# An induced-attention and ELU feed-forward kernel: one unsplit pair of a block becomes a split one on GpSimd, and the other's subtraction moves to ScalarE

## The chip, the cores and the metric

The kernel runs as one program on one core of a Trainium2 chip. The metric is the time of one execution on the device, in microseconds (us); lower is better. A core has TensorE (PE in the profile, with its weight loads as PEld), VectorE (DVE), ScalarE (ACT), GpSimd (POOL) and SyncE (SP, which issues the transfers here). Each engine works through its own list of instructions in order, and waits on semaphores for the others.

## The reference

Two parts follow each other. The first attends from 32 inducing points to all 12480 tokens of a batch, and then from the tokens back to the 32 results. The second is a feed-forward layer with ELU on all 4 x 12480 tokens.

```python
# attention: B, N, m, C = 4, 12480, 32, 128
h = mab(I, x)          # softmax(scale * I @ x^T) @ x, per batch
x = mab(x, h)          # softmax(scale * x @ h^T) @ h
# feed-forward: d_model 128, d_ff 2048 (weights are float64 inputs)
h = x @ w_in
g = np.where(h > 0.0, h, np.exp(np.minimum(h, 0.0)) - 1.0)
return (g @ w_out).astype(np.float32)
```

## The kernel before, in words

**Blocks, pairs and units.** The tokens of a batch are cut into 25 blocks: 15 of 512 tokens and 10 of 480 (`GROUPING`), 100 blocks in all. d_ff is 16 chunks of 128; two chunks are a pair, so a block has 8 pairs. One pair of one block is a unit, numbered n = 0 to 799; n modulo 8 is its place in the block.

**One unit.** `ffn_in` (L560, L568): two matmuls fill a tile `ph` of [128, 2, T] in PSUM with h + 1, and ScalarE writes e = exp(ph - 1) to SBUF. `ffn_mid` (L574): VectorE forms min(max(ph, 1), e), which is ELU + 1. `ffn_split` (L583 to L597) subtracts the 1 and, for most pairs, cuts the value into a rounded upper part `gh` and a lower part `gl`, each of which one fast matmul can carry. `ffn_out` (L618) adds the products with w_out into the block's `po` in PSUM. After the eighth pair VectorE transposes `po` (L625), and SP stores it.

**Three kinds of pair.** `PLAN` gives a letter to each of the 8 pairs; `PLAN_CALM` replaces it for the last 17 blocks of the last batch (block 8 on), where no next batch is being prepared. The kinds differ in who makes what:

- D: ELU + 1 stays in `ph`; ScalarE writes `gh` (L583), VectorE writes `gl` (L586) and only then is `ph` free. Six matmuls for the output.
- P: ELU + 1 goes to `e`, so `ph` is free after L574; ScalarE writes `gh`, then GpSimd subtracts 1 in place (L591) and writes `gl` (L596). Six matmuls.
- N: ELU + 1 goes to `e`; GpSimd subtracts 1 in place (L591). There is no split: two matmuls in full float32 with `wo_n`, each of which the profile records twice.

**Buffers.** The pools rotate: 3 tiles of `ph` (PSUM), 5 of `e` (`EB`), 4 of `gh` (`GHB`), 3 of `gl` (`GLB`). A split pair's `gl` takes the buffer of the third split pair before it, and so waits for that pair's output matmuls. Which `ph` tile a unit takes is settled when the program is built.

**What sets the order.** TensorE's order is written out by hand (`manual_schedule`): input matmuls of unit n, then output matmuls of unit n - 5 (`LAG`), then n + 1 and n - 4. Attention steps of this batch and of the next (`attend`, `first_half`) are put between units at written-out times. The order on VectorE, ScalarE and GpSimd is chosen when the program is built, by a scheduler with a timeline of its own; it decides, for example, whether a D pair's L586 stands ahead of a later unit's L574.

## Time and profile before

| what | value |
|---|---|
| median of 3 runs (lowest to highest) | 1762.04 us (1761.57 to 1762.32) |
| profiled execution, its span | 1761.6 us, 1759.5 us |
| granted TensorE clock, mean | 0.987 |
| PE busy / PEld busy | 1659.5 us (94%) / 1177.4 us (67%) |
| DVE busy | 1551.8 us (88%) |
| ACT busy | 1425.0 us (81%) |
| POOL busy | 1331.7 us (76%) |

Busy means that an instruction was recorded as running. A matmul's record is longer than the time until the next one can start, since they are pipelined, so the distance between starts tells more than a matmul's length. The chain of waits is the work followed back from the last instruction: at each step to what released it. "Idle before <- X" names the instruction whose end let the waiting one start.

### The profile page before, as it was taken

Reading aid. Unit: us, or ns where it says so; the run is one execution under the profiler, and the core shown is the slowest. Engines: PE = TensorE matmul, PEld = TensorE weight load, DVE = VectorE, ACT = ScalarE, POOL = GpSimd, SP = SyncE. Lnnn points to the kernel's source line nnn. Section 1 sums busy time; section 2 is a strip of 40 time slices with the busy share of each in tenths; the row PEclk is TensorE's granted clock in tenths of the full one; section 3 lists DMA queues with packets and bytes.
Section 4 is the critical chain, followed back from the end, with each engine's and each line's share of the span. In section 5 each row is a group of like instructions: output and inputs, shape, how many; then the busy total and the mean of one; then the engine's idle time right before and its main releaser. Section 6 shows DMA issues by size and latency. Waiting matters only on the chain.

```text
span 1759.5 us, 22797 instructions
## 1 busy us (share of the span) xinstructions
PE 1659.5 (94%) x7480; PEld 1177.4 (67%) x7480; DVE 1551.8 (88%) x1635; ACT 1425.0 (81%) x1662; POOL 1331.7 (76%) x955
## 2 busy tenths in 40 slices
PE   6699999999999999999999999999999999989897
PEld 4356666677766766767676666667777776667676
DVE  6899989888999898889899998988899988888886
ACT  6778888788887887878787888878888888888786
POOL 3978877777787777777787787777778887766665
PEclk9599999999999999999999999999999999999999
DMA  7362323323234224232225232321221211111111
GB/s 248 65 98 48 66 56 51 73 44 78 53 54 72 60 49 77 41 53 71 66 42 88 44 65 60 52 49 41 58 53 18 45 22 32 25 23 34 21 17 17
DMA packets 384757, 98.12 MB, mean 56 GB/s; under 512 B 364864, under 2 KB 370784, under 8 KB 384384
## 3 DMA queue, kind: packets, MB, share of 16 engines
q1 hardware_dynamic: 384640, 96.68, 28.4%
q8 instruction: 59, 0.97, 0.2%
q14 instruction: 58, 0.48, 0.1%
HBM read 48.94 MB, written 25.56 MB: 42 GB/s over the span
## 4 chain that ended last, share of the span: by engine, by line
PE 73%; DVE 12%; ACT 5%; issue 3%; POOL 3%; DMA 3%; SPq 0%; DVEq 0%; ACTq 0%; POOLq 0%
PE po L618 51%; PE ph L560 18%; DVE gl L586 4%; ACT e L568 3%; DVE ph L574 2%; DVE e L574 2%; DVE xT L241 2%; ACT gh L583 1%; PE ps_hh L369 1%; PE ps_t L485 1%; PE ps_s L293 1%; POOL gl L596 1%; DMA w_raw<-in_moe_w_in_dram 1%; DMA xq<-in_x_dram 1%; DMA xm<-in_x_dram 1%
## 5 line engine op out<-in xcount | busy, mean ns | idle before, releaser
L568 ACT ACTIVATE e<-ph 128x1024 f32<-128x1024 f32 (+1 forms) x800 | 803.5, 1005 | 241.3 <-PE ph L560 237.9
L591 POOL TENSOR_SCALAR e<-e 128x1024 f32<-128x1024 f32 (+1 forms) x483 | 495.4, 1031 | 354.2 <-ACT gh L583 309.0
L596 POOL TENSOR_TENSOR gl<-e,gh 128x1024 fp32r<-128x1024 f32 (+1 forms) x300 | 704.4, 2348 | 19.8 <-PE po L618 0.9
L574 DVE SCALAR_TENSOR_TENSOR e<-ph,e 128x1024 f32<-128x1024 f32 (+1 forms) x483 | 571.5, 1187 | 75.1 <-ACT e L568 73.1
L560 PE MATMUL ph<-stk,hw 128*128 128x512 f32 (+1 forms) x1600 | 563.0, 433 | 60.7 <-DVE gl L586 43.7
L618 PE MATMUL po<-gh,wo_h 128*128 128x512 f32 (+1 forms) x1234 | 481.7, 390 | 10.5 <-ACT e L568 6.5
L618 PE MATMUL po<-gh,wo_l 128*128 128x512 f32 (+1 forms) x1234 | 478.9, 388 | 0.0
L560 PEld LDWEIGHTS ph<-stk,hw 128*128 128x128 f32 x1600 | 289.9, 189 | 247.1 <-issue 92.8
L574 DVE SCALAR_TENSOR_TENSOR ph<-ph,e 128x1024 f32<-128x1024 f32 (+1 forms) x317 | 378.3, 1196 | 47.7 <-ACT e L568 46.4
L586 DVE SCALAR_TENSOR_TENSOR gl<-ph,gh 128x1024 fp32r<-128x1024 f32 (+1 forms) x317 | 375.8, 1185 | 40.4 <-PE po L618 25.9
L618 PE MATMUL po<-gl,wo_h 128*128 128x512 f32 (+1 forms) x1234 | 379.1, 388 | 2.8 <-POOL gl L596 2.8
L618 PE MATMUL po<-e,wo_n 128*128 128x512 f32 (+1 forms) x732 | 336.3, 582 | 0.0
L583 ACT ACTIVATE gh<-e 128x1024 fp32r<-128x1024 f32 (+1 forms) x300 | 311.1, 1037 | 26.6 <-DVE e L574 21.9
L583 ACT ACTIVATE gh<-ph 128x1024 fp32r<-128x1024 f32 (+1 forms) x317 | 318.0, 1003 | 11.5 <-DVE ph L574 9.7
L618 PEld LDWEIGHTS po<-gh,wo_h 128*128 128x128 f32 x1234 | 232.4, 188 | 64.5 <-ACT s L302 5.6
L618 PEld LDWEIGHTS po<-gl,wo_h 128*128 128x128 f32 x1234 | 232.4, 189 | 49.1 <-POOL gl L596 3.9
L618 PEld LDWEIGHTS po<-gh,wo_l 128*128 128x128 f32 x1234 | 232.7, 189 | 46.3 <-issue 0.2
L618 PEld LDWEIGHTS po<-e,wo_n 128*128 128x128 f32 x732 | 138.1, 189 | 97.3 <-issue 84.0
L625 DVE STREAM_TRANSPOSE o<-po 128x512 f32<-128x512 f32 (+1 forms) x100 | 69.3, 693 | 11.8 <-PE po L618 11.8
L241 DVE STREAM_TRANSPOSE xT<-xq 128x1024 f32<-128x1024 f32 (+2 forms) x39 | 45.2, 1160 | 0.0
L369 PE MATMUL ps_hh<-xm,e 128*32 128x128 f32 (+2 forms) x872 | 33.3, 296 | 8.4 <-DVE bias L326 2.3
L369 PEld LDWEIGHTS ps_hh<-xm,e 128*32 128x32 f32 (+2 forms) x872 | 25.4, 117 | 20.1 <-issue 12.4
(94 smaller groups left out, 582.3 us busy)
## 6 DMA issues: line engine op xcount, KB each, us to landing
xm<-in_x_dram SPq DMA_DIRECT2D x32, 512.0 KB, 4.4
out_dram<-o SPq DMA_DIRECT2D x240, 64.0 KB, 2.0
xq<-in_x_dram SPq DMA_DIRECT2D x84, 128.0 KB, 3.6
out_dram<-o SPq DMA_DIRECT2D x160, 60.0 KB, 2.0
stk<-ahi SPq DMA_DIRECT2D x118, 64.0 KB, 2.0
xq<-in_x_dram SPq DMA_DIRECT2D x60, 120.0 KB, 3.4
stk<-ahi SPq DMA_DIRECT2D x80, 60.0 KB, 2.0
stk<-alo SPq DMA_DIRECT2D x59, 64.0 KB, 2.0
```

Source lines behind the costliest of these rows:

```text
L241: tc.keep_in_program_order(nc.vector.transpose(t, xq.rearrange("p u d -> p (u d)")))
L293: nc.tensor.matmul(ps[j * Q : (j + 1) * Q, :T], indT, block_xT(b, g0 + j), start=True, stop=True,)
L369: nc.tensor.matmul(ps[c * Q : (c + 1) * Q, :C], st["e", g][:np_, u * Q : (u + 1) * Q], st["xm", g, u - u % UP][:np_, u % UP, :], start=(u ...
L560: nc.tensor.matmul(ph[:, i], state[b]["hw"][:, f * P : (f + 1) * P], stacks[b, k], start=True, stop=True,)
L568: nc.scalar.activation(e, ph, AF.Exp, bias=-1.0)
L574: nc.vector.scalar_tensor_tensor(out=v["g"], in0=v["ph"], scalar=1.0, in1=v["e"], op0=ALU.max, op1=ALU.min)
L583: nc.scalar.activation(v["gh"], v["g"], AF.Copy, bias=-1.0)
L586: nc.vector.scalar_tensor_tensor(out=v["gl"], in0=v["g"], scalar=-1.0, in1=v["gh"].bitcast(F32), op0=ALU.add, op1=ALU.subtract,)
L591: nc.gpsimd.tensor_scalar(out=v["e"], in0=v["e"], scalar1=-1.0, scalar2=1.0, op0=ALU.add, op1=ALU.mult)
L596: nc.gpsimd.tensor_sub(v["gl"], v["e"], v["gh"].bitcast(F32))
L618: nc.tensor.matmul(po[:, :T], w, g, start=(cp == 0 and i == 0), stop=(cp == NCP - 1 and i == len(parts) - 1),)
L625: nc.vector.transpose(o.rearrange("p u d -> p (u d)"), po[:, :T])
```

## The change

`PLAN` goes from PDNPDPND to PDPDPNPD: three P, three D and two N become four P, three D and one N, in another order. `PLAN_CALM` goes from PDNPDPDD to PDPDDNPD: three P, four D and one N as before, in another order. The N pair's subtraction of 1 goes from GpSimd to ScalarE (a Copy with bias -1, in place on `e`); the P pair's instructions are the same. The tables `CHUNKS_N` and `CHUNKS_S` follow the plans: `wo_n` now holds two chunks and not four.

```diff
-PLAN = "PDNPDPND"
-PLAN_CALM = "PDNPDPDD"
+PLAN = "PDPDPNPD"
+PLAN_CALM = "PDPDDNPD"
...
                 out=v["gl"], in0=v["g"], scalar=-1.0, in1=v["gh"].bitcast(F32),
                 op0=ALU.add, op1=ALU.subtract,
             )
-        else:
+        if how == "N":
+            nc.scalar.activation(v["e"], v["e"], AF.Copy, bias=-1.0)
+        if how == "P":
             nc.gpsimd.tensor_scalar(
                 out=v["e"], in0=v["e"], scalar1=-1.0, scalar2=1.0, op0=ALU.add, op1=ALU.mult
             )
-        if how == "P":
             v["gl"] = glp.tile(shape, F32R, tag="gl", name=f"gl_{n}")
             nc.gpsimd.tensor_sub(v["gl"], v["e"], v["gh"].bitcast(F32))
```

The lines behind the edit move by one: L591 is now the ScalarE Copy, L593 and L597 are GpSimd's two steps, L619 the output matmuls and L626 the transpose of `po`.

The order on VectorE is shown for block 37, units 296 to 303, a block of 512 tokens in the second batch (a name such as `ph_297_6324` is the tile `ph` of unit 297). L574 writing `e` is a P or N pair, L574 writing `ph` a D pair, L586 a D pair's lower part. Before:

```order
L574 SCALAR_TENSOR_TENSOR e_296_6309<-ph_296_6306,e_296_6309 128x1024
L586 SCALAR_TENSOR_TENSOR gl_295_6320<-ph_295_6295,gh_295_6318 128x1024
L574 SCALAR_TENSOR_TENSOR ph_297_6324<-ph_297_6324,e_297_6327 128x1024
L574 SCALAR_TENSOR_TENSOR e_298_6344<-ph_298_6341,e_298_6344 128x1024
L586 SCALAR_TENSOR_TENSOR gl_297_6355<-ph_297_6324,gh_297_6353 128x1024
L574 SCALAR_TENSOR_TENSOR e_299_6365<-ph_299_6362,e_299_6365 128x1024
L574 SCALAR_TENSOR_TENSOR ph_300_6371<-ph_300_6371,e_300_6374 128x1024
```

And now, from the same unit on (L626 is the transpose of the block before):

```order
L574 SCALAR_TENSOR_TENSOR e_296_6603<-ph_296_6600,e_296_6603 128x1024
L586 SCALAR_TENSOR_TENSOR gl_295_6614<-ph_295_6581,gh_295_6612 128x1024
L574 SCALAR_TENSOR_TENSOR ph_297_6618<-ph_297_6618,e_297_6621 128x1024
L574 SCALAR_TENSOR_TENSOR e_298_6638<-ph_298_6635,e_298_6638 128x1024
L586 SCALAR_TENSOR_TENSOR gl_297_6645<-ph_297_6618,gh_297_6643 128x1024
L574 SCALAR_TENSOR_TENSOR ph_299_6652<-ph_299_6652,e_299_6655 128x1024
L626 STREAM_TRANSPOSE o_1_11_6680<-po_1_11_6555 128x512
L574 SCALAR_TENSOR_TENSOR e_300_6672<-ph_300_6669,e_300_6672 128x1024
```

The lower part of unit 297 (place 1) stands at the same place. Counting split pairs back from it, its buffer was unit 293's before (296, 295, 293; 294 was an N) and is unit 294's now (296, 295, 294). Behind it now stand the D pair of unit 299 and the transpose, and then unit 300, whose `ph` tile unit 302 takes.

The order on ScalarE in the same block, from the middle to the end; L568 is the exponential, L583 an upper part. Before:

```order
L568 ACTIVATE e_300_6374<-ph_300_6371 128x1024
L583 ACTIVATE gh_299_6389<-e_299_6365 128x1024
...
L568 ACTIVATE e_301_6400<-ph_301_6397 128x1024
L583 ACTIVATE gh_300_6410<-ph_300_6371 128x1024
L568 ACTIVATE e_302_6417<-ph_302_6414 128x1024
L583 ACTIVATE gh_301_6426<-e_301_6400 128x1024
L568 ACTIVATE e_303_6434<-ph_303_6431 128x1024
L568 ACTIVATE e_304_6443<-ph_304_6440 128x1024
```

And now:

```order
L568 ACTIVATE e_301_6697<-ph_301_6694 128x1024
L583 ACTIVATE gh_299_6687<-ph_299_6652 128x1024
...
L583 ACTIVATE gh_300_6707<-e_300_6672 128x1024
L568 ACTIVATE e_302_6715<-ph_302_6712 128x1024
L591 ACTIVATE e_301_6697<-e_301_6697 128x1024
L568 ACTIVATE e_303_6728<-ph_303_6725 128x1024
L583 ACTIVATE gh_302_6737<-e_302_6715 128x1024
L568 ACTIVATE e_304_6745<-ph_304_6742 128x1024
```

Before, two exponentials followed each other where a pair was an N; now each exponential has a second ScalarE step in its block, an upper part or the Copy. On GpSimd the order before was two steps for each P and one for each N; now it is two steps for each of the four P pairs, evenly in every second unit.

## The prediction, on record before the result was known

> **What bounds the kernel now.** I read the cores first, then the chain of waits, then the busy time by stage.

> ```profile
> core 0: 1759.5 us, clock 0.987
> ...
> PE 73%; DVE 12%; ACT 5%; issue 3%; POOL 3%; DMA 3%; SPq 0%; DVEq 0%; ACTq 0%; POOLq 0%
> ...
> 200.00:1300.00 1100.00, 1072.98 (x4863) 755.47 (x4862) 989.52 (x1023) 899.34 (x1020) 854.40 (x584) 1.00 0.31 58
> 1300.00:1455.00 155.00, 155.00 (x622) 112.98 (x621) 141.44 (x140) 133.55 (x147) 130.85 (x89) 1.00 0.19 33
> 1460.00:1740.00 280.00, 251.28 (x1027) 187.32 (x1026) 238.32 (x230) 229.13 (x251) 190.85 (x125) 0.99 0.14 24
> ...
> ACT e L568 <- PE ph L560: 237.9, 281, 2.3
> ```

> The windows' columns are PE, PEld, DVE, ACT, POOL, granted clock, DMA share and GB/s. PE is busy 97.5% of the long middle (1072.98 of 1100) and all of 1300 to 1455; DVE 90 to 91%, ACT 82 to 86%, POOL 78 to 84%. The chain is PE for 73%, and ScalarE's main wait is for PE. So PE bounds the blocks up to 1455 us; the calm blocks behind have PE at 90% (251.28 of 280) and another bound, below.

> **What the change takes from PE.** The chain shows units back to back, a split pair's output as x6 and an N pair's as x4 (records), with the input matmuls between:

> ```profile
> 702.04 1.38 PE po L618 x6
> 703.89 1.40 PE po L618 x6
> 705.74 1.72 PE po L618 x4
> 707.46 0.47 PE ph L560 x2
> 707.92 1.38 PE po L618 x6
> ...
> 787.81 1.30 PE po L618 x6
> 789.54 1.61 PE po L618 x4
> 791.59 1.31 PE po L618 x6
> ```

> At 512 tokens a split unit takes 1.85 us from start to start (702.04 to 703.89) and an N unit 2.18 (705.74 to 707.92): the swap saves 0.33. At 480 it saves 2.05 - 1.73 = 0.32. The plan is used in 83 blocks (three batches and 8 blocks): 53 of 512, 30 of 480. 53 x 0.33 + 30 x 0.32 = **27 us less on PE**. The calm plan keeps one N and saves nothing. [...]

> **What it adds to ScalarE.** Per plan block one upper part and one Copy, both reading SBUF like `gh<-e`:

> ```profile
> 700.29 1.03 ACT L568 ACTIVATE e<-ph 128x1024 f32<-128x1024 f32 x1 [0.21 <-PE ph L560]
> 701.22 1.02 ACT L583 ACTIVATE gh<-ph 128x1024 fp32r<-128x1024 f32 x1
> 702.12 1.03 ACT L568 ACTIVATE e<-ph 128x1024 f32<-128x1024 f32 x1
> 703.03 1.07 ACT L583 ACTIVATE gh<-e 128x1024 fp32r<-128x1024 f32 x1
> 703.99 1.03 ACT L568 ACTIVATE e<-ph 128x1024 f32<-128x1024 f32 x1
> ...
> 708.02 1.03 ACT L568 ACTIVATE e<-ph 128x1024 f32<-128x1024 f32 x1 [1.16 <-PE ph L560]
> ```

> Back to back an exponential takes 0.92, `gh<-ph` 0.90, `gh<-e` 0.96. A D and a P unit together need 3.70 (700.29 to 703.99), what PE takes for two split units (2 x 1.85). Today ScalarE recovers at each N: 1.16 idle at 708.02. The new N unit has a second step too, so what is left in a block is about 2.18 - 1.88 = 0.3. Per block ScalarE gets 1.9 more, 83 x 1.9 = 158, and 17 x 0.93 = 16 in the calm blocks: busy 1425 to 1599. The cover is the 237.9 us that it waits for PE. **Bounds:** nothing, if that cover holds in place; at most what the rival below gives. Queued behind ScalarE are the exponentials that release `ph`; there is not much room, so I take a third of the upper bound of 53 (worked out with that rival): **+18 us**.

> **What it adds to GpSimd.** One P more, two N steps fewer:

> ```profile
> 704.19 1.05 POOL L591 TENSOR_SCALAR e<-e 128x1024 f32<-128x1024 f32 x1 [0.16 <-ACT gh L583]
> 705.32 2.38 POOL L596 TENSOR_TENSOR gl<-e,gh 128x1024 fp32r<-128x1024 f32 x1
> 707.65 1.07 POOL L591 TENSOR_SCALAR e<-e 128x1024 f32<-128x1024 f32 x1
> ```

> A P costs 3.46 (704.19 to 707.65), an N 1.05: +1.36 a block, busy 1332 to about 1427. Four P need 13.8 of the some 15.1 us that a block's PE work lasts, one in every second unit (3.46 of 3.70). It fits: zero, unless attention steps pile up on it.

> **The buffers of the lower parts: the added wait.** Before, every D of the plan had an N among the three units ahead, so its `gl` buffer came from the unit four back, whose output was long done. Now places 1, 2, 3 and 4 take the buffer of the unit three back. For P pairs and place 3 that is no later than their own work. For place 1 it is. Unit 297 is a D at place 1:

> ```profile
> 701.41 0.63 PE L560 MATMUL ph<-stk,hw 128*128 128x512 f32 x2
> ...
> 706.19 1.21 DVE L586 SCALAR_TENSOR_TENSOR gl<-ph,gh 128x1024 fp32r<-128x1024 f32 x1
> 707.32 1.21 DVE L574 SCALAR_TENSOR_TENSOR e<-ph,e 128x1024 f32<-128x1024 f32 x1
> 709.08 1.23 DVE L574 SCALAR_TENSOR_TENSOR ph<-ph,e 128x1024 f32<-128x1024 f32 x1 [0.55 <-ACT e L568]
> 710.22 0.71 DVE L625 STREAM_TRANSPOSE o<-po 128x512 f32<-128x512 f32 x1
> 710.85 0.67 DVE L360 STREAM_TRANSPOSE e<-s 128x512 f32<-128x512 f32 x1
> ```

> Its L586 ran at 706.19; the output of unit 294 ended at 707.46 (the chain's row above). Waiting for it, L586 starts 1.3 later, and VectorE, in order, stands. Lay it out from unit 297's input at 701.58 in the chain's timing as 0: output of 294 ends 5.88; L586 to 7.06 (1.13 to the next start); unit 299's L574 to 8.20; the transpose to 8.83 (0.63); unit 300's L574 ends 10.05 (1.22). Unit 302 takes that `ph` tile and is due at 4 x 1.85 + 2.18 = 9.58. PE stands **0.5 us**. That order (L586, place 3, transpose, place 4) is in 27 of the 83 blocks. In 14, place 3 comes ahead of L586, and the same sum gives 0.26. In the others nothing: without the transpose it ends at 9.42. 27 x 0.5 + 14 x 0.26 = **+17 us**. Bounds: 0, where attention matmuls stand between; 42, if all 83 lose 0.5.

> **The calm blocks.** They show today what such a buffer does:

> ```profile
> DVE gl L586 <- PE po L618: 15.2, 13, 1.3
> PE ph L560 <- DVE gl L586: 28.7, 31, 3.1
> ...
> 1581.91 0.70 PE L560 MATMUL ph<-stk,hw 128*128 128x480 f32 x2 [1.41 <-DVE gl L586]
> 1586.06 0.70 PE L560 MATMUL ph<-stk,hw 128*128 128x480 f32 x2 [0.24 <-DVE gl L586]
> ...
> 1582.71 0.97 ACT L568 ACTIVATE e<-ph 128x960 f32<-128x960 f32 x1 [0.80 <-PE ph L560]
> 1583.71 1.17 DVE L574 SCALAR_TENSOR_TENSOR ph<-ph,e 128x960 f32<-128x960 f32 x1 [0.21 <-ACT e L568]
> ```

> (The first two rows are waits in 1460 to 1740.) A block loses 1.41 + 0.24. In the changed program place 6 takes, in 15 of 17 blocks, the `ph` tile of place 5 just ahead of it: input to the end of L574 is 1584.88 - 1581.91 = 2.97, against a unit of 1.73, so PE would stand 1.3. Per block 0.35 less, 5 us; two D in a row may cost some back (bounds -5 to +10). I take **-3 us**.

> **Sum**, against the profiled execution's 1761.6 (median 1762.0, so no correction): 1761.6 - 27 + 18 + 17 - 3 = **1767 us**.

> **Rivals.**

> *The relief stays, the waits are absorbed.* Attention matmuls stand between units in most blocks and hide 0.5, and ScalarE's idle time covers its two steps. For it: PE is the bound and ScalarE waits for it, 237.9 us. Against it: DVE stays at 90% of a shorter block. 1761.6 - 27 - 3 with half of the 17: **1740 us**.

> *ScalarE becomes the bound.* Windowed rows give its load:

> ```profile
> L568 ACT ACTIVATE e<-ph 128x1024 f32<-128x1024 f32 x301 | 309.0, 1027 | 93.0 <-PE ph L560 92.7
> L568 ACT ACTIVATE e<-ph 128x960 f32<-128x960 f32 x224 | 217.7, 972 | 69.0 <-PE ph L560 67.7 <-issue 0.2
> ```

> 525 exponentials in 200 to 1300 are 65.6 blocks, 16.76 us each, 13.7 of it ScalarE's; with 1.87 more, 15.57. The highest share that any of the three elementwise engines keeps over a stretch is DVE's 141.44 of 155, 91.2%. Were that the most for ScalarE too, a block takes 17.07, 0.31 more, 83 x 0.31 = 26: **1788 us**, which is 53 above 1735, the time without any stall. It decides as soon as ScalarE cannot go above 93% (15.57 of 16.76). For GpSimd the same reckoning, (13.02 + 1.36) / 0.912 = 15.8, is under 16.76: no bound.

> *The bubble is in every block.* The lower part's wait costs 0.5 in all 83, 42 in place of 17: **1791 us**. Speaking for it: the calm rows repeat theirs in block after block. [...] Against it: only 27 blocks have the bad order.

> **How the numbers follow.** The forecast of a small loss has 0.46 (its own range 1759 to 1782), the absorbed case 0.34, ScalarE as bound 0.10, the bubble everywhere 0.10. 0.2%, 3.5 us, is about what a measurement of this kernel tells from no change. Faster: 0.31 of the absorbed case and 0.03 of the forecast, 0.34. Same: 0.03 and 0.10, 0.13. Slower: 0.33 + 0.20, 0.53. The range reaches from 1737, where nearly all stalls are absorbed, to 1800, just above the two dear cases.

> **What would show it.** N records of L619 in the plan halve; ScalarE's busy time near 1599 and GpSimd's near 1427. The wait of VectorE's lower part for PE's output, now 15.2 in the calm stretch, appears in the plan blocks, some 40 to 80 times of about 1 us. PE's waits at the input matmuls name VectorE's L574. If ScalarE bounds, its wait for PE falls to a few tens of us and PE waits on exponentials. The prediction is wrong if PE keeps 97.5% in the middle with fewer N (absorbed), or if GpSimd's `gl` appears among PE's waits.

## The result, and the profile after

| | before | after |
|---|---|---|
| median (lowest to highest) of 4 runs | 1762.03 us (1761.57 to 1762.32) | 1785.77 us (1784.76 to 1786.33) |
| ratio, with its 95% interval | | 1.0136 (1.0121 to 1.0151) |
| span of the profiled execution, granted clock | 1759.5 us, 0.987 | 1783.8 us, 0.988 |

The changed kernel is 23.7 us slower. The forecast was 1767, slower by 5; the time lies inside the range of 1737 to 1800, 19 us above the forecast and close to the two dear rivals (1788 and 1791).

The page of the changed kernel, busy time of each engine, and the shares of the chain of waits:

```profile
span 1783.8 us, 23710 instructions
...
PE 1653.0 (93%) x7646; PEld 1200.5 (67%) x7646; DVE 1548.6 (87%) x1635; ACT 1586.2 (89%) x1843; POOL 1428.9 (80%) x938
...
PE 58%; DVE 18%; ACT 10%; issue 8%; POOL 4%; DMA 1%; DVEq 0%; SPq 0%; ACTq 0%; POOLq 0%
```

PE's share of the chain fell from 73% to 58%, and VectorE's and ScalarE's rose from 12 and 5 to 18 and 10. PE has a little less to do than before (1653.0 against 1659.5 busy), and the chain hangs on it less.

The groups of the page that belong to the swap (busy time, mean ns of one, idle time ahead):

```profile
L619 PE MATMUL po<-gl,wo_h 128*128 128x512 f32 (+1 forms) x1400 | 430.0, 388 | 4.7 <-POOL gl L597 4.6
...
L619 PE MATMUL po<-e,wo_n 128*128 128x512 f32 (+1 forms) x400 | 183.6, 581 | 0.0
L591 ACT ACTIVATE e<-e 128x1024 f32<-128x1024 f32 (+1 forms) x100 | 103.1, 1031 | 13.6 <-DVE e L574 13.5
```

Before, the first two rows had x1234 and x732. So the change does what it says: 83 units more are split, each with two such records, 83 fewer are full float32, and 100 Copies have come to ScalarE.

Where the 24 us came from is read by stage. I call the time from the first input matmul of unit 0 to that of unit 664 the **plan stage** (the 83 blocks that use `PLAN`), and what is behind it the **rest**. The starts of those two units, before and then after:

```profile
68.54 1.22 PE L560 MATMUL ph<-stk,hw 128*128 128x512 f32 x2 [9.35 <-DVE stk L528]
...
1455.57 1.03 PE L560 MATMUL ph<-stk,hw 128*128 128x512 f32 x2
```

```profile
68.52 1.22 PE L560 MATMUL ph<-stk,hw 128*128 128x512 f32 x2 [9.01 <-DMA hw<-hw_l]
...
1482.76 0.63 PE L560 MATMUL ph<-stk,hw 128*128 128x512 f32 x2
```

The plan stage went from 1387.0 to 1414.2 us (+27.2), the rest from 303.9 to 301.0 (-2.9). Two windows over just the two plan stages (columns as in the prediction), before and after:

```profile
68.52:1455.52 1387.00, 1351.06 (x5981) 950.48 (x5982) 1249.93 (x1282) 1139.58 (x1288) 1089.17 (x751) 1.00 0.30 56
```

```profile
68.52:1482.72 1414.20, 1343.79 (x6148) 973.82 (x6149) 1247.23 (x1282) 1286.62 (x1455) 1204.33 (x752) 1.00 0.30 55
```

PE's busy time there fell by 7.3, and the time in which it stood rose from 35.9 to 70.4. What it waited for shows in the waits of the changed kernel (engine, tile and line waited for; us in total, times, longest):

```profile
ACT e L568 <- PE ph L560: 92.7, 156, 2.5
...
PE ph L560 <- DVE e L574: 61.3, 85, 1.7
...
DVE gl L586 <- PE po L619: 58.7, 60, 1.3
...
POOL gl L597 <- PE po L619: 29.9, 45, 1.4
```

VectorE's lower part now waits for PE's output 60 times, 58.7 us (before 26 times, 25.9 us, half of them in the calm blocks), and PE waits at its input matmuls for VectorE's L574, 61.3 us (before 6.1). Counted off in the order of the records, 39 of VectorE's 44 waits in the plan stage are at place 1; 26 of GpSimd's 40 there, 26.4 us, are at place 2. ScalarE's wait for PE fell from 237.9 to 92.7, but was not used up. Block 37, the one that the prediction laid out, shows the two waits together. Its VectorE rows, from the L574 of unit 298 to those of units 300 and 301 (one row, x2):

```profile
715.15 1.23 DVE L574 SCALAR_TENSOR_TENSOR e<-ph,e 128x1024 f32<-128x1024 f32 x1 [0.18 <-ACT e L568]
717.66 1.23 DVE L586 SCALAR_TENSOR_TENSOR gl<-ph,gh 128x1024 fp32r<-128x1024 f32 x1 [1.28 <-PE po L619]
718.80 1.22 DVE L574 SCALAR_TENSOR_TENSOR ph<-ph,e 128x1024 f32<-128x1024 f32 x1
719.93 0.71 DVE L626 STREAM_TRANSPOSE o<-po 128x512 f32<-128x512 f32 x1
720.56 2.32 DVE L574 SCALAR_TENSOR_TENSOR e<-ph,e 128x1024 f32<-128x1024 f32 x2
```

and PE's row for the input of unit 302:

```profile
721.89 0.70 PE L560 MATMUL ph<-stk,hw 128*128 128x512 f32 x2 [0.67 <-DVE e L574]
```

L586 waits 1.28 for the output of the unit three back, the three instructions queued behind it (unit 299's L574, the transpose, unit 300's L574) run late without a gap, and PE stands 0.67 until the last of them has freed `ph`. Predicted were 1.3 and 0.5.

### The profile page after: what moved, and what is told of

Its sections match the earlier page's. It is cut to its first block, busy times and chain, and to the rows that moved or that the text cites. A ratio compares the mean times of both kernels' runs of the same rounds, so it can differ in the third digit from the quotient of the medians.

```text
span 1783.8 us, 23710 instructions
## 1 busy us (share of the span) xinstructions
PE 1653.0 (93%) x7646; PEld 1200.5 (67%) x7646; DVE 1548.6 (87%) x1635; ACT 1586.2 (89%) x1843; POOL 1428.9 (80%) x938
## 4 chain that ended last, share of the span: by engine, by line
PE 58%; DVE 18%; ACT 10%; issue 8%; POOL 4%; DMA 1%; DVEq 0%; SPq 0%; ACTq 0%; POOLq 0%
PE po L619 38%; PE ph L560 15%; DVE e L574 6%; ACT e L568 6%; DVE ph L574 4%; DVE gl L586 3%; ACT gh L583 3%; DVE o L626 1%; POOL gl L597 1%; PE ps_s L293 1%; DVE xT L241 1%; PE ps_hh L369 1%; PE ps_t L485 1%; PE ps_x L261 1%; POOL e L593 1%
## 5 line engine op out<-in xcount | busy, mean ns | idle before, releaser
L597 POOL TENSOR_TENSOR gl<-e,gh 128x1024 fp32r<-128x1024 f32 (+1 forms) x383 | 900.2, 2351 | 56.0 <-PE po L619 29.9
L568 ACT ACTIVATE e<-ph 128x1024 f32<-128x1024 f32 (+1 forms) x800 | 801.0, 1003 | 98.7 <-PE ph L560 92.7
L574 DVE SCALAR_TENSOR_TENSOR e<-ph,e 128x1024 f32<-128x1024 f32 (+1 forms) x483 | 569.5, 1184 | 77.7 <-ACT e L568 74.6
L560 PE MATMUL ph<-stk,hw 128*128 128x512 f32 (+1 forms) x1600 | 544.9, 422 | 89.7 <-DVE e L574 61.3
L593 POOL TENSOR_SCALAR e<-e 128x1024 f32<-128x1024 f32 (+1 forms) x383 | 394.1, 1029 | 238.3 <-ACT gh L583 230.5
L619 PE MATMUL po<-gh,wo_h 128*128 128x512 f32 (+1 forms) x1400 | 546.4, 390 | 12.1 <-ACT e L568 9.8
L619 PE MATMUL po<-gh,wo_l 128*128 128x512 f32 (+1 forms) x1400 | 543.2, 388 | 0.0
L560 PEld LDWEIGHTS ph<-stk,hw 128*128 128x128 f32 x1600 | 281.5, 189 | 282.5 <-DVE e L574 82.9
L586 DVE SCALAR_TENSOR_TENSOR gl<-ph,gh 128x1024 fp32r<-128x1024 f32 (+1 forms) x317 | 376.1, 1186 | 71.6 <-PE po L619 58.7
L619 PE MATMUL po<-gl,wo_h 128*128 128x512 f32 (+1 forms) x1400 | 430.0, 388 | 4.7 <-POOL gl L597 4.6
L574 DVE SCALAR_TENSOR_TENSOR ph<-ph,e 128x1024 f32<-128x1024 f32 (+1 forms) x317 | 379.0, 1196 | 49.1 <-ACT e L568 48.7
L583 ACT ACTIVATE gh<-e 128x1024 fp32r<-128x1024 f32 (+1 forms) x383 | 398.4, 1040 | 19.4 <-DVE e L574 7.0
L583 ACT ACTIVATE gh<-ph 128x1024 fp32r<-128x1024 f32 (+1 forms) x317 | 318.7, 1005 | 1.5 <-DVE ph L574 1.0
L619 PEld LDWEIGHTS po<-gh,wo_h 128*128 128x128 f32 x1400 | 263.3, 188 | 75.0 <-ACT e L568 13.2
L619 PEld LDWEIGHTS po<-gl,wo_h 128*128 128x128 f32 x1400 | 263.6, 188 | 56.8 <-POOL gl L597 5.5
L619 PEld LDWEIGHTS po<-gh,wo_l 128*128 128x128 f32 x1400 | 263.9, 189 | 51.1 <-issue 0.2
L619 PE MATMUL po<-e,wo_n 128*128 128x512 f32 (+1 forms) x400 | 183.6, 581 | 0.0
L591 ACT ACTIVATE e<-e 128x1024 f32<-128x1024 f32 (+1 forms) x100 | 103.1, 1031 | 13.6 <-DVE e L574 13.5
L619 PEld LDWEIGHTS po<-e,wo_n 128*128 128x128 f32 x400 | 75.6, 189 | 53.1 <-issue 45.8
L626 DVE STREAM_TRANSPOSE o<-po 128x512 f32<-128x512 f32 (+1 forms) x100 | 69.1, 691 | 3.3 <-PE po L619 3.2
L515 POOL TENSOR_TENSOR s<-s,sm 128x512 f32<-128x512 f32 (+3 forms) x28 | 28.7, 1027 | 16.1 <-DVE sm L514 16.1
```

Source lines behind the costliest of these rows:

```text
L515: eng.tensor_tensor(out=s, in0=s, in1=sm.unsqueeze(2).broadcast_to([np_, U, Q]), op=ALU.mult)
L560: nc.tensor.matmul(ph[:, i], state[b]["hw"][:, f * P : (f + 1) * P], stacks[b, k], start=True, stop=True,)
L568: nc.scalar.activation(e, ph, AF.Exp, bias=-1.0)
L574: nc.vector.scalar_tensor_tensor(out=v["g"], in0=v["ph"], scalar=1.0, in1=v["e"], op0=ALU.max, op1=ALU.min)
L583: nc.scalar.activation(v["gh"], v["g"], AF.Copy, bias=-1.0)
L586: nc.vector.scalar_tensor_tensor(out=v["gl"], in0=v["g"], scalar=-1.0, in1=v["gh"].bitcast(F32), op0=ALU.add, op1=ALU.subtract,)
```

## The experiments

All times are medians of the profiled and timed runs of each kernel; ratios are against the kernel before on the same chip, with a 95% interval. "Plan" and "rest" are the two stages, from each kernel's own trace.

| run | what it is | median us | ratio | plan us | rest us |
|---|---|---|---|---|---|
| before | | 1762.0 | 1 | 1387.0 | 303.9 |
| after | | 1785.8 | 1.0136 (1.0121 to 1.0151) | 1414.2 | 301.0 |
| e1_control | after, `SB` 4 | 1786.0 | 1.0135 (1.0120 to 1.0150) | 1415.4 | 300.7 |
| e2_glb4 | and a fourth `gl` buffer | 1754.9 | 0.9956 (0.9941 to 0.9971) | 1396.3 | 289.0 |
| e3_before_n_on_act | before, N subtractions on ScalarE | 1788.0 | 1.0143 (1.0128 to 1.0158) | 1413.8 | 303.7 |
| e4_no_copy | after, no N subtraction | 1775.6 | 1.0076 (1.0059 to 1.0093) | 1409.1 | 295.9 |
| e5_light_glb3 | ScalarE as light as before, 3 buffers | 1777.0 | 1.0086 (1.0071 to 1.0101) | 1411.3 | 296.3 |
| e6_light_glb4 | the same, 4 buffers | 1728.5 | 0.9814 (0.9798 to 0.9831) | 1373.0 | 286.0 |
| e7_before_glb4 | before, 4 buffers | 1734.4 | 0.9845 (0.9831 to 0.9860) | 1390.6 | 274.1 |
| e8_plan_n_on_pool | after's plans, N subtraction on GpSimd | 1775.8 | 1.0080 (1.0065 to 1.0095) | 1407.9 | 297.8 |
| e9_own_place1 | after, place 1 has a `gl` tile of its own | 1756.4 | 0.9967 (0.9954 to 0.9980) | 1398.0 | 289.0 |
| e10_own_place3 | after, place 3 has one | 1793.9 | 1.0182 (1.0167 to 1.0197) | 1431.6 | 294.4 |
| e11_glb4_n_on_pool | e8 with 4 buffers | 1742.5 | 0.9889 (0.9874 to 0.9904) | 1385.4 | 288.4 |
| e12_rotated_plan | e11 with other plans | 1724.6 | 0.9788 (0.9772 to 0.9804) | 1377.8 | 277.4 |

### A fourth buffer for the lower parts: e1_control, e2_glb4, e7_before_glb4

A fourth `gl` buffer takes room in SBUF (4 KB a partition, 1024 float32), which two of the six buffers of another pool (`SB`, 512 float32 each) give up. e1 makes only that smaller, e2 adds the buffer, and e7 does both to the kernel before.

```diff
-    GLB = 3
-    SB = 6
+    GLB = 4     # e1: stays 3
+    SB = 4
```

> The changed kernel with the pool of attention scores cut from 6 to 4 tiles, which makes room for a fourth lower-part buffer; the order of TensorE and SyncE is the same. Every theory: 1786 us, within 0.3%, since those scores are read long before their tile is needed again. It is the baseline for e2.

> The same with four lower-part buffers instead of three: a split pair's gl then takes the buffer of the fourth split pair before it. Theory A (the missing lower-part buffer costs most of the 0.66 us of new standing time per plan block): the wait of VectorE's lower part for PE's output nearly goes, the plan blocks get back 0.4 to 0.6 us each (33 to 50 us), and the calm blocks also lose their 1.3 us stall (up to 20 us): 1720 to 1750 us. Theory B (ScalarE's load costs it): the plan blocks stay within 0.1 us of what they were and only the calm blocks gain: 1765 to 1772 us.

> The kernel before with four lower-part buffers (scores pool of 4). Its plan blocks have no lower part that waits for the unit three back, so they stay at 1387 us from the first input to the calm stretch; the calm blocks lose their stall of 1.65 us in 15 blocks, 12 to 25 us: 1738 to 1750 us. Compared with the change and four buffers (1755) it tells what the change costs when buffers are no matter: if it is ScalarE's load, this one is faster by 5 to 15 us.

The smaller pool costs nothing (1786.0 against 1785.8). The buffer takes 31 us from the changed kernel: 19 in the plan stage, 12 in the rest. In e2's waits, neither VectorE's nor GpSimd's lower part waits for PE's output any more. Block 37 of e2, VectorE again:

```profile
706.72 1.22 DVE L574 SCALAR_TENSOR_TENSOR e<-ph,e 128x1024 f32<-128x1024 f32 x1 [0.19 <-ACT e L568]
707.86 1.21 DVE L586 SCALAR_TENSOR_TENSOR gl<-ph,gh 128x1024 fp32r<-128x1024 f32 x1
708.99 1.22 DVE L574 SCALAR_TENSOR_TENSOR ph<-ph,e 128x1024 f32<-128x1024 f32 x1
710.99 0.72 DVE L626 STREAM_TRANSPOSE o<-po 128x512 f32<-128x512 f32 x1 [0.77 <-PE po L619]
711.63 1.18 DVE L574 SCALAR_TENSOR_TENSOR e<-ph,e 128x1024 f32<-128x1024 f32 x1
```

L586 follows at once. Of the 1.28 that it had waited, 0.77 comes back at the transpose, which needs the whole `po`; so even without the buffer's wait VectorE has to stand in this order, later and for less.

In the kernel before, the same buffer brings nothing in the plan stage (+3.6) and 30 us in the calm blocks, where its L586 did wait. With four buffers on both sides the change is still 20 us slower (1754.9 against 1734.4): 6 in the plan stage and 15 in the calm blocks, whose new order is then worse than the old one (e11, which has that order and four buffers but no Copy on ScalarE, still takes 288.4 there). The buffer is a large cost of the change, but not all that speaks against it.

### The load on ScalarE: e3_before_n_on_act, e4_no_copy, e8_plan_n_on_pool

e3 puts the same load on the kernel before: its two N subtractions of a block go to ScalarE, 16 steps a block as after, and nothing else changes.

```diff
-        else:
+        if how == "N":
+            nc.scalar.activation(v["e"], v["e"], AF.Copy, bias=-1.0)
+        if how == "P":
             nc.gpsimd.tensor_scalar(
```

> The kernel before, with its own plans, and only the subtraction of both N pairs moved from GpSimd to ScalarE: ScalarE's busy time rises by about 1.9 us per plan block as in the change, every lower part keeps the buffer of the unit four back, TensorE's work is that of before. Theory A: as before, 1758 to 1768 us. Theory B: slower by most of what the change lost, 18 to 50 us: 1780 to 1812 us.

e3 alone loses 26 us, 27 of it in the plan stage: as much as the whole change, with no lower part that waits longer. That is above the 18 of the prediction and far below its upper bound of 53. e4 and e8 take one of the two added steps away again, by leaving the N subtraction out (e4) or by giving it back to GpSimd (e8).

```diff
-        if how == "N":
-            nc.scalar.activation(v["e"], v["e"], AF.Copy, bias=-1.0)
-        if how == "P":     # e4: this line stays
+        if how != "D":     # e8
             nc.gpsimd.tensor_scalar(
```

> The changed kernel without any subtraction of 1 for the N pair (its two chunks enter the output as ELU + 1: that work is left out). ScalarE loses 0.95 us per block, 95 us in all; buffers and plans are those of the change. Theory A: 1780 to 1787 us. Theory B: about half of ScalarE's added load goes, and with it half or more of the 24 us: 1762 to 1774 us.

> The changed plans alone: the N pair's subtraction stays on GpSimd, which then has four P of 3.46 and one step of 1.05, 14.9 us a block, and attention steps of about 1 on top, 15.9 of 17; ScalarE has 15 steps. If GpSimd is what counts: 1790 to 1810 us, with its lower parts among TensorE's waits. If ScalarE's Copy is what counts: as without the Copy, 1770 to 1778 us. If only the buffer: 1784 to 1787 us.

In the changed kernel the step is worth only 5 to 6 us of plan stage (1414.2 to 1409.1 and 1407.9), and 10 us in all. It makes no difference whether GpSimd does the subtraction or nobody does: at three buffers, this step on GpSimd costs nothing.

### Both causes in a table of two by two: e5_light_glb3, e6_light_glb4

Both kernels take ScalarE back to its 14 steps of a plan block: no Copy, and the P pair at place 6 uses a constant tile as its upper part in place of its own L583. It also takes no `gh` buffer there, six a block in place of seven, so these come free a little earlier too.

```diff
-        if how != "N":
+        if units[n][2] == 6 and how == "P":
+            v["gh"] = wo_h[:, :8, :].rearrange("p a c -> p (a c)")[:, : 2 * T]...
+        elif how != "N":
             v["gh"] = ghp.tile(shape, F32R, tag="gh", name=f"gh_{n}")
...
-        if how == "N":
-            nc.scalar.activation(v["e"], v["e"], AF.Copy, bias=-1.0)
```

> The changed kernel (scores pool of 4, three lower-part buffers) with ScalarE's load put back to 14 steps a block: no Copy for the N pair, and the P pair at place 6 takes a constant tile as its upper part in place of an L583 of its own (its output products use that constant: that work is left out). GpSimd and TensorE do what the change does, VectorE too. If the bubble of the lower part's buffer alone made up the loss once ScalarE is relieved: 27 us of TensorE's saving less the bubble's 17 to 30 gives 1755 to 1765 us. If the two effects only hide each other (whichever is later sets the end): no better than the kernel without the Copy, 1770 to 1776 us.

> The same with four lower-part buffers: neither ScalarE's added load nor the buffer is left, only TensorE's saving, GpSimd's added load and the new order. If these two causes are the whole of the new standing time, the plan blocks take 27 us less than before and the calm blocks 15 to 20 less: 1715 to 1725 us. If GpSimd or VectorE hold it too: 1735 to 1750 us.

The plan stage of the four, against 1387.0 before:

| | 3 buffers | 4 buffers |
|---|---|---|
| 16 steps on ScalarE | 1414 | 1396 |
| 14 steps on ScalarE | 1411 | 1373 |

From the corner with neither cause (1373), the buffer alone adds 38, ScalarE's load alone adds 23, and both together 41 (42 by e1, which has the small `SB` of the other three). Some 5 of the 23 are spells of half clock in e2 (last section). The two do not add up: where the buffer already makes VectorE late, the two steps cost 3 more. This fits e4 and e8, which showed so little.

The windows of the plan stage show where PE stands, e5 and then e6:

```profile
68.52:1479.82 1411.30, 1340.28 (x6154) 977.36 (x6149) 1259.29 (x1282) 1151.19 (x1287) 1201.96 (x749) 1.00 0.29 55
```

```profile
68.52:1441.52 1373.00, 1333.01 (x6152) 978.27 (x6152) 1253.58 (x1283) 1147.29 (x1289) 1204.24 (x751) 1.00 0.30 57
```

PE stands 71.0 us in e5 and 40.0 in e6, near the 35.9 of before. The waits for the buffer, e5 and then e6:

```profile
DVE gl L591 <- PE po L622: 23.2, 27, 1.6
...
POOL gl L600 <- PE po L622: 40.2, 74, 1.9
```

```profile
DVE gl L591 <- PE po L622: 0.2, 1, 0.2
```

In e5 GpSimd's lower parts wait more than VectorE's; in the prediction they were to be no later than their own work.

### Which place it is: e9_own_place1, e10_own_place3

Both give one lower part of VectorE a tile of its own; the other lower parts keep the three that rotate. In both the number of buffers is four. Counting back, e9 leaves no lower part with the buffer of the unit three back; in e10 places 1 and 2 still have it.

```diff
+    glo = ctx.enter_context(tc.tile_pool(name="glo", bufs=1))
...
-            v["gl"] = glp.tile(shape, F32R, tag="gl", name=f"gl_{n}")
+            pool, tag = (glo, "glo") if units[n][2] == 1 else (glp, "gl")   # e10: == 3
+            v["gl"] = pool.tile(shape, F32R, tag=tag, name=f"gl_{n}")
```

> The changed kernel (scores pool of 4) with a tile of its own for the lower part of the D pair at place 1; all other split pairs rotate over the three others, each at least four units apart. If any lower part three units back is what costs: as with four buffers, 1750 to 1760 us. If it is not the wait of these tiles but the room as a whole: above 1770 us.

> The same memory, with the own tile given to the D pair at place 3 instead. Places 1 and 2 still take the buffer of the unit three back, places 3 and 4 no longer. If place 1 is the culprit, as the prediction had it: most of the loss stays in the plan blocks, 1405 to 1414 us from the first input to the calm stretch, 1775 to 1786 us in all. If place 3 (or 4) is: as with four buffers, 1750 to 1760 us.

The tile for place 1 does all that the fourth buffer does (1756.4 against 1754.9, the rest 289.0 in both). The tile for place 3 does not: place 1 still waits for the unit three back, as this row of block 37 of e10 shows, and the plan stage is even 17 us longer than after's.

```profile
723.66 1.22 DVE L588 SCALAR_TENSOR_TENSOR gl<-ph,gh 128x1024 fp32r<-128x1024 f32 x1 [1.28 <-PE po L621]
```

So it is the place that counts, and not how many tiles there are. Places 3 and 4 are not what costs; 1 and 2 are, and these two runs do not part them. That it is place 1 is read from the traces: in the changed kernel PE waits for VectorE's steps behind place 1, as in block 37, while it waits for a lower part of GpSimd only once, 4.6 us, within the first 100 us. Of e10's 17 us, 15 are in the seven blocks that hold a spell of half clock (last section).

### Versions that beat both: e11_glb4_n_on_pool, e12_rotated_plan

e11 is e8 with `SB` 4 and `GLB` 4: 15 steps on ScalarE and four buffers. e12 also turns the plan so that the block begins with a D, and gives the calm blocks the old order.

```diff
-PLAN = "PDPDPNPD"
-PLAN_CALM = "PDPDDNPD"
+PLAN = "DPNPDPDP"
+PLAN_CALM = "PDNPDPDD"
```

> The changed plans with four lower-part buffers and the N pair's subtraction on GpSimd: ScalarE 15 steps a block, GpSimd 14.9 us of them. Between four buffers with the Copy (1755) and four buffers with ScalarE at 14 steps (1729), if ScalarE's load counts step by step: 1738 to 1746 us. If GpSimd is too full: above 1755 us.

> A try at something faster than both kernels: four lower-part buffers, the calm plan of before, and the change's plan turned so that its one N stands at place 2 as in that calm plan (DPNPDPDP), subtraction on GpSimd. If the plan blocks are those of the run before (about 1383 us) and the calm blocks those of the kernel before with four buffers (274 us): 1722 to 1732 us.

e11 is faster than the kernel before (1742.5), but not than that kernel with four buffers (1734.4). e12, at 1724.6, is: 2.1% under the kernel before and some 10 us under e7. Its plan stage is 13 us shorter than e7's, and its calm blocks give back 3. The middle of its plan stage:

```profile
200.00:1300.00 1100.00, 1065.16 (x5034) 785.61 (x5035) 1008.41 (x1033) 965.41 (x1095) 1017.16 (x658) 1.00 0.32 59
```

VectorE, ScalarE and GpSimd are busy 91.7, 87.8 and 92.5% there, and PE 96.8%. So the idea of fewer full float32 pairs does pay, if the step that it adds is on GpSimd, the buffers are there and the order suits.

## Why the prediction was right or wrong

**That it is slower, and by what: right.** The relief on PE is less than the new standing, and the chain in block 37 is the predicted one, with its sizes (1.28 of wait for 1.3, 0.67 of standing for 0.5). The busy times came as said: ScalarE 1586 (1599 predicted), GpSimd 1429 (1427). VectorE's lower part waits outside the calm stretch some 45 times (60 in all, less 15 in 1460 to 1740), where 40 to 80 were predicted, and nearly all at place 1. It waited there before too, 13 times (26 less 13), so the output of the unit four back was not always done. Of the two signs of being wrong neither came: PE is busy 95.4% of the middle and not 97.5%, and no lower part of GpSimd is among its waits after the first 100 us.

**PE's saving of 27: as a price right, as a gain only in part.** The unit starts of PE in e6, where little stands in the way:

```profile
708.19 0.61 PE L560 MATMUL ph<-stk,hw 128*128 128x512 f32 x2
...
710.02 0.61 PE L560 MATMUL ph<-stk,hw 128*128 128x512 f32 x2
...
711.85 0.61 PE L560 MATMUL ph<-stk,hw 128*128 128x512 f32 x2
...
715.87 0.61 PE L560 MATMUL ph<-stk,hw 128*128 128x512 f32 x2
```

A split unit takes 1.83, and the N unit with the split one behind it 4.02, so the N unit 2.19 and the swap 0.36, as predicted or a little more. Yet the plan stage of e6 is only 14 us under the one before: PE's busy time is 18 less and its standing 4 more. Most of the other 13 is standing as well, and half of that does not show as idle. An N unit of block 48, before and in e6:

```profile
894.54 1.77 PE L618 MATMUL po<-e,wo_n 128*128 128x480 f32 x4
895.77 0.97 PE L560 MATMUL ph<-stk,hw 128*128 128x480 f32 x2
896.58 0.38 PE L618 MATMUL po<-gh,wo_h 128*128 128x480 f32 x1
```

```profile
890.47 1.77 PE L622 MATMUL po<-e,wo_n 128*128 128x480 f32 x4
892.27 0.70 PE L560 MATMUL ph<-stk,hw 128*128 128x480 f32 x2
892.82 0.39 PE L622 MATMUL po<-wo_h 128*128 128x480 f32 x1
```

From the first row to the third it is 2.04 before and 2.35 in e6: PE's input comes 0.31 late, and no idle time is shown, because the record of the N unit's last matmul runs on meanwhile. Read from such distances between starts (an estimate, good to a microsecond or two), 74 input matmuls of e6's plan stage come late, 41 us in all, and 42 of the kernel before, 30 us; 41 and 25 of them stand behind VectorE's L574. So the relief was there, and some 11 us of it went into waits for VectorE that neither priced cause makes. Whether the new order or GpSimd's fourth P pair makes VectorE late there was not tried. With the whole 27 as relief, the standing that the change added in the plan stage is 27.2 + 27 = 54 us, where the prediction had 18 + 17 = 35. That is 19 us, as much as the forecast missed: 13 here, and 6 in the two terms that follow.

**The lower-part buffer, +17: right on top of ScalarE's load, too small alone.** On top of that load it costs 18 (e2 against after). Alone it costs 38 (e5 against e6), more than twice the term, and near the 42 of the rival that put a bubble into every block. But VectorE does not wait in every block; it is 45 waits and not 83. The prediction took the loss of a single unit in a block with the bad order, 0.5 or 0.26. The runs show two things beside that. The lower parts of GpSimd wait as well (29.9 us after, 40.2 in e5), most of it at place 2, which the prediction ruled out. And PE stands more often at `ph` than there are bad orders: 70 times outside the calm stretch, 43 us (61.3 less 18.1, 85 times less 15; before 8 times in all). A single bad place was priced, and the places behind it were taken as undisturbed.

**ScalarE, +18: right as a middle, wrong as a term of a sum.** By itself the load costs 23 (e2 against e6) to 27 (e3 against before). An estimated 5 and 9 of these are spells of half clock, three in e2 and five in e3 (last section), so its waits alone come to 18 in both. Beside the buffer's wait it costs 3 to 5 (e5 and e4). The prediction added the two terms as if each had PE's time to itself. In fact both make the same thing late, the release of `ph`, and the smaller one hides under the larger. By the runs the sum is 1387 - 27 + 38 + 3 + 13, or, the two taken in the other order, 1387 - 27 + 23 + 18 + 13. Together they cost 41, and the prediction had 35. That it came so near is luck in part: each priced alone, as the prediction meant to, they would have made 61.

**GpSimd, nothing: right for the step itself.** Putting the N subtraction on GpSimd costs nothing against leaving it out (e8, e4). Whether the P pair that it gained has a part in the 13 is open.

**The calm blocks, -3: right, in part by luck.** The rest is 2.9 shorter. Without the Copy on ScalarE it is 295.9 (e4) or 297.8 (e8), so the Copy costs 3 to 5 us there, for which the prediction had no term, and the new order gained more than the 5 that it had. Where no attention step stands in the block, PE stands about 1.25 at place 6; 1.3 was predicted:

```profile
1635.78 0.71 PE L560 MATMUL ph<-stk,hw 128*128 128x480 f32 x2 [1.26 <-DVE e L574]
...
1652.05 0.71 PE L560 MATMUL ph<-stk,hw 128*128 128x480 f32 x2 [1.25 <-DVE e L574]
```

**The rivals.** *Absorbed* (1740) did not come. Even without the two causes (e6, where the added work on ScalarE is left out) the plan stage gains 14 and not 27; the other 18 that bring e6 to 1728.5 come in the rest, where it has the fourth buffer. *ScalarE as the bound* (1788) gave nearly the measured time by the wrong mechanism: it waited for PE for 92.7 us still, and its supposed ceiling of 91.2% is not one, since it was busy 93.1% of 1300 to 1455 in the changed kernel itself (144.38 of 155), and the same 16 steps fill 92.1% of the middle of e2:

```profile
200.00:1300.00 1100.00, 1065.75 (x4987) 774.26 (x4987) 983.25 (x1024) 1013.34 (x1149) 946.34 (x583) 1.00 0.30 58
```

With that load as the bound, four buffers would not have made the blocks shorter. *The bubble in every block* (1791) is nearest in size, and right in that the wait costs more than its count of bad orders says.

## What to carry to other kernels

When two waits make the same resource late (here `ph`), price the larger and add little for the smaller; to learn the size of each, take both away and put each back, since taking away one alone shows only what the other leaves. When a plan turns unsplit work into split work, count for each place how far back its buffer now lies and whether that unit's reader is done by then: one tile, given at place 1, was worth 30 us here (1786.0 to 1756.4), and at place 3 it gained nothing (1793.9). A wait shorter than the tail of the matmul ahead showed in the distance between starts and not as idle time (0.31 us at the N unit of block 48 in e6): an estimated 41 us of late inputs in e6 had 28 us of idle time. And a buffer that the change makes scarce has to be given to the kernel before too, ahead of a verdict: with four buffers the old kernel gained 28 us and the change was still the slower one.

## What the runs showed of the hardware that was not expected

**A standstill of PE that costs more than itself.** In e3 and e10 some blocks lose far more than others. In e3 the plan's blocks of 512 tokens are as long as before in the median (16.61 against 16.57), and the loss sits in a few, where a stall that was there has grown. One of them, PE before:

```profile
636.22 0.73 PE L560 MATMUL ph<-stk,hw 128*128 128x512 f32 x2 [1.22 <-DVE gl L586]
```

The same place in e3, and the windows around it:

```profile
643.51 0.73 PE L560 MATMUL ph<-stk,hw 128*128 128x512 f32 x2 [1.81 <-DVE gl L586]
```

```profile
640.00:644.00 4.00, 2.19 (x10) 1.50 (x9) 4.00 (x5) 3.48 (x5) 2.67 (x2) 1.00 0.64 99
644.00:648.00 4.00, 4.00 (x9) 2.04 (x8) 2.85 (x3) 1.97 (x2) 1.98 (x2) 0.59 0.58 115
648.00:652.00 4.00, 3.97 (x18) 1.98 (x18) 2.53 (x3) 3.47 (x5) 1.86 (x2) 0.98 0.07 13
```

PE starts again at 643.51, and for the next 4 us its granted clock is 0.59: it is busy all the time, but nine matmuls are recorded where eighteen are in the next window. The clock that is missing, 0.41 x 4 and 0.02 x 4, at half speed (0.50 in the spell of the kernel before, below) is 3.28 + 0.16, so about 3.4 us at 0.5, or 1.7 us lost. From 100 us on, the plan stage of e3 has five such spells, that of e10 seven, of e2 three, of e9 two and of e11 one; the other kernels, the one before and the changed one among them, have none there. Over the whole plan stage the granted clock is 0.99 in e2, e3 and e9, and 1.00 in the kernel before, the changed one, e5, e6 and e7. A stall of e10, and the two windows behind it (PE's busy time, clock, DMA):

```profile
796.65 0.74 PE L621 MATMUL po<-gh,wo_h 128*128 128x480 f32 x1 [1.84 <-DVE bias L327]
```

```profile
796.00:800.00 4.00, 3.35 (x9) 0.58 0.44 66
800.00:804.00 4.00, 4.00 (x20) 0.99 0.13 29
```

Two blocks of e10 with spells took 19.20 and 20.60 us in place of 17.28 and 17.95 after; seven spells at 1.7 us are some 12 of its 17 us. In e3 five are some 9 of its 27, and in e2 three some 5. That its other losses come from the added load is what the edit says; why they gather in a few blocks was not tried.

The two stalls shown are 1.81 and 1.84 us, while the waits of the changed kernel's PE, of which the longest at `ph` is 1.7 us from 150 us on, were followed by no spell between 150 and 1760 us (clock 1.00 from 85.65 to 1782.07). So for this kernel a stall that grows from 1.2 to 1.8 us can cost not 0.6 but an estimated 2.3, the 1.7 of the spell with it.

```profile
1647.33:1650.74 3.41, 0.64 (x3) 1.00 0.00 0
1650.74:1654.15 3.41, 3.07 (x8) 0.50 0.00 0
114.74:118.15 3.41, 1.62 (x6) 1.00 1.22 163
```

```profile
1546.56:1549.97 3.41, 1.71 (x8) 1.00 0.37 55
```

PE was idle for 2.77 us ahead of the spell, and for 1.79 and 1.70 in the two that no spell followed. In e9 PE waits for VectorE's L494 three times for the same 1.81 us; below them is the stretch behind the second:

```profile
460.05 0.46 PE L621 MATMUL po<-gh,wo_h 128*128 128x480 f32 x1 [1.81 <-DVE s L494]
...
879.06 0.68 PE L621 MATMUL po<-gh,wo_h 128*128 128x480 f32 x1 [1.81 <-DVE s L494]
...
1299.36 0.46 PE L621 MATMUL po<-gh,wo_h 128*128 128x480 f32 x1 [1.81 <-DVE s L494]
...
879.12:882.53 3.41, 3.41 (x9) 0.50 0.62 112
```

The second lies whole in the stretch that ends at 879.12. The first and the third are cut by a border (459.28 and 1298.96, 123 times 3.413 us from 879.12), into 1.04 and 0.77 and into 1.41 and 0.40, and no spell follows. Nor does one follow a stall of 2.68 us in e3, up to 529.90, that is cut into 1.45 and 1.23 (clock 1.00 in 528 to 532 and in 532 to 536). So a spell followed the stall of 1.81 us that lay in one stretch, and none followed those of 1.81 and 2.68 us that were cut in two.
